# Two of the first four loads of a gated-attention and gMLP kernel asked for by ScalarE instead of SyncE

## The chip, the cores and the metric

The kernel runs on one core of a Trainium2 chip. The core has five engines with an instruction stream each: TensorE (PE in the profile, its weight loads PEld), VectorE (DVE), ScalarE (ACT), GpSimd (POOL) and SyncE (SP). All DMA transfers of the core share 16 DMA engines. The metric is the device time of one launch in microseconds (us), as the median of several runs.

## The reference

Two layers run one after the other. The first is a recurrence over 768 positions for 4 batches and 8 heads with a head width of 48:

```python
for t in range(S):
    state = alpha[:, :, t, :, None] * state + einsum('bhd,bhe->bhde', k[:, :, t], v[:, :, t])
    y[:, :, t] = einsum('bhd,bhde->bhe', q[:, :, t], state)
```

The second is a gated MLP with mixing over positions, on `x`, which is `y` with the heads laid side by side (768 positions of 384 numbers for each batch):

```python
h = maximum(x @ w_in, 0)                     # 384 -> 1024
u, v = h[..., :512], h[..., 512:]
v_n = (v - mean(v)) / sqrt(var(v) + 1e-6)    # over the 512
v_s = einsum('ts,bsd->btd', w_spatial, v_n) + b_spatial[None, :, None]
out = (u * v_s) @ w_out                      # 512 -> 384
```

Inputs and output are float32.

## The kernel before

The recurrence is computed in chunks of 128 positions, six to a batch, 24 in all. The first eight chunks are taken two at a time (`pair(j)`, for j from 0 to 3); the others go through `first(i)` one by one. For a pair, position 2p lies in the first half and position 2p+1 in the second half of partition p.

A pair begins with four loads, one each of `alpha` (tile `ac`), `k` (`kc`), `q` (`qc`) and `v` (`vc`), all through the inner function `load`. Each brings 384 KB, as rows of 96 numbers (384 bytes): 8 heads on 128 partitions. The tiles of a name rotate over three buffers. The steps of a pair that follow are:

- `ln` on ScalarE (L446) takes the logarithm of `ac` into `la`. It waits for the load of alpha.
- `cum` on TensorE (L455) sums the logarithms up to each position with a triangular matrix, into two PSUM banks.
- `einv` and `eexp` on ScalarE (L463, L472) take exp of minus the sums into `binvp` and exp of the sums in place.
- `ktf` (L477) multiplies `kc` by `binvp` into `kt`, twice, once for each half. In the first pair GpSimd does it. It waits for `binvp` and for the load of k.
- `qtf` on VectorE (L484) multiplies `qc` by exp of the sums into `qt`, twice. It waits for the load of q.
- `vbf` turns `vc` into bfloat16 (`vbp`), one half on GpSimd (L200) and one on ScalarE (L198), the lines of a copying helper. It waits for the load of v.
- TensorE transposes `qt` and `kt` (L505); VectorE and ScalarE copy the results to `kqT` (L200, L198).
- `upd` on TensorE (L539, L547) makes the state's increments from `kt` and `vbp`; VectorE then begins the state (L331), and ScalarE and GpSimd go on with it (L553, L338).
- The scores (L577), their masking on VectorE (L588) and the outputs (L604, L617) follow; the result goes through `x_sb` to `xT`, from which the second layer's matmuls (L822) start.

The order on each engine is written out by hand in the string `PLAN`. A word names an engine and an operation's number: P is TensorE, D is VectorE, A is ScalarE, G is GpSimd, S is SyncE, and Q marks the point at which a load has landed, which emits nothing. The function `replay` emits the operations in that order, and each engine works through its own list strictly. Numbers after a colon are columns of filler matmuls on the tile `junk` (L188), which TensorE runs ahead of the operation.

In `PLAN`, operations 34, 36, 38 and 40 are the issues of alpha, k, q and v for pair 0; 94, 96, 98 and 100 are those for pair 1; 42 is the first `ln`. All loads and stores are issued by SyncE, except the 1.5 KB of `b_spatial` by GpSimd. Completions of the loads are counted on eight semaphores in turn, so the ninth load waits on SyncE until the first has landed. The words around the change are:

```python
G32 S34 Q33 S36 G0 S38 S40 Q35 D1 Q37 S94 A42 D2 Q39 S96 P43:512:512:192 P53:64 A44 A45 G46
```

Ahead of the first `ln`, ScalarE has only the load of its function table (L171).

Of the kernel before, what the change touches and what calls it, by code (L numbers as in the profile page):

```python
# [54 lines left out]
LETTERS = {"P": "PE", "D": "DVE", "A": "ACT", "G": "POOL", "S": "SP", "Q": "DMA"}  # L55

PLAN = """
G32 S34 Q33 S36 G0 S38 S40 Q35 D1 Q37 S94 A42 D2 Q39 S96 P43:512:512:192 P53:64 A44 A45 G46 Q41 S98 A54 A55 D47 G56
D57 P51:512 Q95 P49 S100 P59:64 P61 A58 G48 D60 A50 D52 P63:192 Q97 S163 A62 P247 D65 A102 P71 D248 P74 D72 A64 Q99
S167 P103:96 G66 P113 D73 A104 A114 D68 D76 A115 Q101 P249 S165 G116 A105 A250 D117 G106 D107 P121:512 Q164 S169 D75  # L60
A122 P111:64 G67 P109 D112 P119 A110 G69 D120 Q168 S4 P131:192 D70 P134 G108 P77 G118 D133 G3 P123:128 A171 Q166
# [63 lines left out]
def kernel(  # L125
# [12 lines left out]
    nc = tc.nc  # L138
# [19 lines left out]
    LD, LP, WT, ST = 1.03, 1.46, 2.35, 0.8  # L158
# [129 lines left out]
    def op(key, *args, **kw):  # L288

        users = kw.pop("use", ())  # L290
        o = Op(key, *args, **kw)
        for s in users:
            s.users.append(o)
        ops.append(o)
        made[key] = o
        return o

    def got(*keys):
        return [made.get(x) for x in keys]

    def dma(key, us, emit, deps, prio, eng="SP", issue=0.99, lat=1.9):
        o = op(key + ("issue",), eng, issue, emit, deps, prio=prio)
        return op(key, "DMA", us, lambda _: None, [o], prio=prio, lat=lat)
# [102 lines left out]
    def io_users(x, j, back=None):  # L406

        j = j - IO if back is None else j
        if x == "cum":
            return got(("cum", 2 * j), ("cum", 2 * j + 1), ("cump", j, 0), ("cump", j, 1), ("updq", j))  # L410
        return got((x, 2 * j), (x, 2 * j + 1), (x + "p", j), (x + "p", j, 0), (x + "p", j, 1))
# [5 lines left out]
    def pair(j):  # L417

        st = T[2 * j]
        P = float(20 * j)  # L420
# [10 lines left out]
        def load(name, src):  # L431
            def emit(_):
                t = st[name] = io_pool.tile([128, 2, H, D], FP32, name=name).rearrange(
                    "p a h d -> p (a h d)").rearrange("p (h a d) -> p h a d", h=H, a=2)
                nc.sync.dma_start(  # L435
                    out=t.rearrange("p h a d -> p h (a d)"),
                    in_=src[b, :, t0:t0 + 2 * C, :].rearrange("h (p a) d -> p h (a d)", a=2))
            return emit

        for n, (x, src, u) in enumerate((("ac", alpha, "ln"), ("kc", k, "kt"), ("qc", q, "qt"), ("vc", v, "vb"))):  # L440
            dma((x, 2 * j), LP, load(x, src), io_users(u, j), P + 0.1 * n, issue=1.48)
            made[(x, 2 * j + 1)] = made[(x, 2 * j)]
            made[(x, 2 * j + 1, "issue")] = made[(x, 2 * j, "issue")]

# [650 lines left out]
    for b in range(B):  # L1095
        for c in range(NCH):
            i = b * NCH + c
            if i // 2 in PAIRS:
                if i % 2 == 0:
                    pair(i // 2)  # L1100
            else:
                first(i)
            second_v(b, c)
            if c == 2 or c == NCH - 1:
                for ft in range(NDS):
                    second_u(b, ft, c // 3)
        if b == 0:
            weights()
            bias()
        for th in range(2):  # L1110
            for dsl in range(NDS):
                second_s(b, dsl, th)
        for tt in range(NT):
            second_o(b, tt)
# [33 lines left out]
```

## Time and profile before

| | |
|---|---|
| median of 3 runs | 145.41 us (144.61 to 146.45) |
| span of the profiled execution, first to last instruction | 142.9 us |
| the profiled execution's own time | its span is what the page gives; 2.5 us less than the median of the runs |
| TensorE busy | 132.9 us (93%) |
| VectorE busy | 122.2 us (85%) |
| ScalarE busy | 108.2 us (76%) |
| GpSimd busy | 86.0 us (60%) |
| SyncE's DMA queue | 88944 packets, 28.32 MB, 92.0% of the 16 DMA engines |
| granted TensorE clock | 1.000 |

The span runs from the first to the last instruction of one profiled execution. The median comes from other executions and takes in what lies around the span. "Busy" adds up the time in which an engine had an instruction under way. A row of the timeline gives start, duration, engine, line of the kernel, operation, output and inputs, and in brackets how long the engine had been idle and what released it. In rows of DMA issues (SPq), the duration is that of the issuing; when the data has landed is told by the time to landing, counted from the start of the issue.

### The profile page before, as it was taken

How to read it: one execution, taken by the hardware profiler on the slowest of the kernel's cores; microseconds unless marked ns; L12 is line 12 of the kernel's file. 1: busy time of each engine (PE TensorE's matmuls, PEld its weight loads, DVE VectorE, ACT ScalarE, POOL GpSimd, SP SyncE). 2: the span in 40 equal slices, each digit the busy share in tenths (PEclk: the TensorE clock that was granted, in tenths of full speed). 3: DMA queues.
4: the chain of work that ended last, by engine and by line, in shares of the span. 5: the costliest groups of instructions: out<-in, count | busy, mean ns of one | idle time of the engine just before them, and what ended most of it. 6: DMA issues, size and time to landing. Idle time of an engine off the chain costs nothing.

```text
span 142.9 us, 4962 instructions
## 1 busy us (share of the span) xinstructions
PE 132.9 (93%) x1910; PEld 83.7 (59%) x1923; DVE 122.2 (85%) x290; ACT 108.2 (76%) x280; POOL 86.0 (60%) x147
## 2 busy tenths in 40 slices
PE   7978977999799999999999999999999999999990
PEld 3464857456465666665655666656666666556460
DVE  6759998998989799989789999889889989776950
ACT  3567398899976799999987889999878688760131
POOL 6945853748317999971288879910999994003700
PEclk9999999999999999999999999999999999999999
DMA  4999989999998999999899999999999103229645
GB/s 115 268 261 265 250 201 327 334 322 328 251 224 163 213 276 161 203 176 198 145 205 192 164 209 162 208 143 206 187 156 222 55 7 137 86 98 338 229 150 180
DMA packets 89000, 28.64 MB, mean 200 GB/s; under 512 B 83728, under 2 KB 87440, under 8 KB 88976
## 3 DMA queue, kind: packets, MB, share of 16 engines
q1 hardware_dynamic: 88944, 28.32, 92.0%
q8 instruction: 15, 0.25, 0.8%
q14 instruction: 9, 0.07, 0.2%
q0 software_dynamic: 32, 0.00, 0.0%
HBM read 23.60 MB, written 4.72 MB: 198 GB/s over the span
## 4 chain that ended last, share of the span: by engine, by line
PE 70%; DMA 10%; SPq 6%; ACT 6%; DVE 3%; issue 2%; ACTq 0%
PE bank L822 50%; DMA ac<-in_alpha_dram 10%; SPq L435 6%; PE bank L748 3%; PE bank L713 3%; PE bank L776 2%; PE bank L660 2%; ACT v_sb L204 2%; PE bank L734 2%; PE bank L770 2%; PE bank L392 2%; DVE stats L887 1%; DVE vn L919 1%; ACT x_sb L198 1%; PE bank L663 1%
## 5 line engine op out<-in xcount | busy, mean ns | idle before, releaser
L822 PE MATMUL bank<-w_spT,vn 128*128 128x384 bf16 x192 | 36.3, 326 | 0.0
L981 POOL TENSOR_TENSOR gT<-vsb,uT 128x384 bf16<-128x384 f32 x28 | 25.8, 928 | 14.2 <-DVE vsb L968 13.5
L822 PEld LDWEIGHTS <-vn 128*128 128x128 bf16 x192 | 16.8, 97 | 10.5 <-DVE vn L919 0.2
L684 POOL TENSOR_TENSOR kt<-kc,binv 128x384 bf16<-128x384 f32 x16 | 14.8, 924 | 12.6 <-ACT bc L679 6.6
L759 DVE TENSOR_TENSOR ptm<-bank,mask 128x512 bf16<-128x512 f32 x32 | 20.8, 683 | 0.6 <-PE bank L748 0.6
L822 PE MATMUL bank<-xT,w_in 128*128 128x384 bf16 x96 | 19.7, 326 | 0.1
L968 DVE TENSOR_TENSOR vsb<-bank,bsp_bc 128x384 f32<-128x384 f32 x31 | 16.6, 552 | 3.0 <-PE bank L822 1.6
L822 PE MATMUL bank<-w_out_sb,gT 128*128 128x384 bf16 (+1 forms) x100 | 18.6, 319 | 0.0
L822 PE MATMUL bank<-w_in,xT 128*128 128x512 bf16 x59 | 16.9, 379 | 1.1 <-issue 0.3
L198 ACT COPY kqT<-bank 128x512 bf16<-128x512 bf16 x26 | 14.8, 592 | 1.3 <-PE bank L713 0.8
L338 POOL TENSOR_TENSOR state<-state,bc 128x192 f32<-128x192 f32 x20 | 10.4, 518 | 8.8 <-ACT bc L553 6.4
L887 DVE BATCH_NORM_STATS2 stats<-v_sb 128x6 f32<-128x512 bf16 x20 | 13.7, 683 | 1.4 <-ACT v_sb L204 1.4
L198 ACT CAST x_sb<-bank 128x384 bf16<-128x384 f32 x24 | 11.5, 485 | 2.2 <-PE bank L776 1.9
L204 ACT ACTIVATE v_sb<-bank 128x512 bf16<-128x512 f32 x20 | 11.6, 601 | 1.6 <-PE bank L822 1.5
L822 PEld LDWEIGHTS <-gT 128*128 128x128 bf16 x100 | 8.9, 97 | 5.6 <-POOL gT L981 0.4
L200 POOL CAST sbd<-state 64x192 bf16<-64x192 f32 x32 | 10.9, 341 | 1.7
L822 PEld LDWEIGHTS <-w_in 128*128 128x128 bf16 x96 | 8.3, 97 | 5.3 <-issue 0.4
L198 ACT COPY xT<-bank 128x192 bf16<-128x192 bf16 (+1 forms) x25 | 8.7, 384 | 2.9 <-PE bank L392 2.6
L919 DVE TENSOR_SCALAR vn<-v_sb,mvs,rstd 128x512 bf16<-128x512 bf16 x24 | 9.8, 437 | 0.7 <-ACT rstd L912 0.7
L588 DVE TENSOR_TENSOR ptm<-bank,mask 128x512 bf16<-128x512 f32 x16 | 10.3, 676 | 0.0
L188 PE MATMUL bank<-junk 128*128 128x512 f32 (+4 forms) x24 | 9.3, 490 | 1.1 <-DVE junk L234 1.1
L200 DVE COPY kqT<-bank 128x512 bf16<-128x512 bf16 x22 | 9.0, 417 | 1.5 <-PE bank L505 0.9
(131 smaller groups left out, 288.2 us busy)
## 6 DMA issues: line engine op xcount, KB each, us to landing
ac<-in_alpha_dram SPq DMA_DIRECT2D x16, 192.0 KB, 4.6
qc<-in_q_dram SPq DMA_DIRECT2D x16, 192.0 KB, 4.7
kc<-in_k_dram SPq DMA_DIRECT2D x16, 192.0 KB, 4.8
vc<-in_v_dram SPq DMA_DIRECT2D x16, 192.0 KB, 4.3
raw_w<-in_moe_w_spatial_dram SPq DMA_DIRECT2D x3, 768.0 KB, 6.8
out_dram<-raw_w SPq DMA_DIRECT2D x11, 192.0 KB, 2.1
out_dram<-o_sb SPq DMA_DIRECT2D x9, 192.0 KB, 2.0
ac<-in_alpha_dram SPq DMA_DIRECT2D x4, 384.0 KB, 6.6
```

The costliest lines, as they stand in the source:

```text
L198: nc.scalar.copy(out=out, in_=in_)
L200: ENG[eng].tensor_copy(out=out, in_=in_)
L204: nc.scalar.activation(out=out, in_=in_, func=AF.Relu)
L338: ENG[eng].tensor_tensor(out=st["state"], in0=st["state"], in1=st["bc"][:, :, None].to_broadcast([128, HP, D]), op=ALU.mult)
L588: nc.vector.tensor_tensor(out=st[f"ptm{par}"][:, s], in0=st[f"pt{s}{par}"], in1=mask2[:, par], op=ALU.mult)
L684: ENG[eng].tensor_mul(out=k_blocks(kt3)[:, :, :, 0:D], in0=quad(st["kc"]), in1=st["binv"])
L759: nc.vector.tensor_tensor(out=st["ptm"][:, s], in0=st[f"pt{s}"], in1=mask4, op=ALU.mult)
L822: return lambda ps: nc.tensor.matmul(out=out(ps), lhsT=lhsT(), rhs=rhs(), start=start, stop=stop)
L887: nc.vector.bn_stats(out=stats, in_=d["v_sb"][:, tt, :])
L919: nc.vector.tensor_scalar(out=d["vn"][:, t, :], in0=d["v_sb"][:, t, :], scalar1=d["mvs"][:, t, 0:1], scalar2=d["rstd"][:, t:t + 1], op0=AL ...
L968: nc.vector.tensor_tensor(out=hold["vs"], in0=ps[:, 0:TH], in1=bsp_bc[:, th, :], op=ALU.add)
L981: ENG[eng].tensor_tensor(out=bt[b]["gT"][:, dsl, cols], in0=hold["vs"], in1=bt[b]["uT"][:, dsl, cols], op=ALU.mult)
```

## The change

The issues of q and v for pair 0 (operations 38 and 40) move from SyncE's list to ScalarE's, where they stand between the table load and the first logarithm. They carry no wait. The loads themselves keep their shape, source and destination. On SyncE the second pair's alpha follows the first pair's k directly. The landing of q is counted on the semaphore that k's landing had, and the other way round. The orders of TensorE, VectorE and GpSimd are unchanged, and lines behind the edit move down by one or two.

```diff
-G32 S34 Q33 S36 G0 S38 S40 Q35 D1 Q37 S94 A42 D2 Q39 S96 P43:512:512:192 P53:64 A44 A45 G46 Q41 S98 A54 A55 D47 G56
+G32 S34 Q33 S36 G0 A38 A40 Q35 D1 Q37 S94 A42 D2 Q39 S96 P43:512:512:192 P53:64 A44 A45 G46 Q41 S98 A54 A55 D47 G56
...
-                nc.sync.dma_start(
+                queue = nc.scalar if j == 0 and name in ("qc", "vc") else nc.sync
+                queue.dma_start(
                     out=t.rearrange("p h a d -> p h (a d)"),
                     in_=src[b, :, t0:t0 + 2 * C, :].rearrange("h (p a) d -> p h (a d)", a=2))
...
-            dma((x, 2 * j), LP, load(x, src), io_users(u, j), P + 0.1 * n, issue=1.48)
+            dma((x, 2 * j), LP, load(x, src), io_users(u, j), P + 0.1 * n, issue=1.48,
+                eng="ACT" if j == 0 and x in ("qc", "vc") else "SP")
```

## The prediction

> **What bounds the kernel now.** I read first the page's slices of the span, then the chain that ended last, then the timeline and the DMA rates of the first 40 us.
>
> ```profile
> PE   7978977999799999999999999999999999999990
> ...
> PEclk9999999999999999999999999999999999999999
> DMA  4999989999998999999899999999999103229645
> ```
>
> Each digit is a tenth of a slice of 3.6 us. From the eleventh slice (about 39 us) TensorE is full to the end. Only before that does it have holes, so a change in the loads can act only through the moment at which the full stretch begins. The chain agrees: from 38.80 us on it is TensorE with small pieces between. Ahead of that it runs over the loads of alpha, ScalarE and VectorE:
>
> ```profile
> 8.65 1.44 SPq L435
> 10.13 7.69 DMA ac<-in_alpha_dram
> 17.87 0.73 issue
> 18.75 0.38 ACT x_sb L198
> 19.17 6.97 DMA ac<-in_alpha_dram
> 26.17 0.84 ACT la L446
> ```
>
> A fixed 104.1 us (38.8 to 142.9) therefore follows whatever the first stretch becomes. How SP issues the first loads (start, duration):
>
> ```profile
> 0.74 0.43 SPq L435 DMA_DIRECT2D ac<-in_alpha_dram  x1
> 1.23 0.57 SPq L435 DMA_DIRECT2D kc<-in_k_dram  x1
> 1.85 1.00 SPq L435 DMA_DIRECT2D qc<-in_q_dram  x1
> 2.89 1.25 SPq L435 DMA_DIRECT2D vc<-in_v_dram  x1
> 4.18 1.45 SPq L435 DMA_DIRECT2D ac<-in_alpha_dram  x1
> ```
>
> The durations grow from 0.43 to 1.45 us for the same shape, so the later ones are not the price of an issue; they are waiting for room. The rates between 0 and 10 us (40 slices of 0.25 us) say for what:
>
> ```profile
> DMA  0000000278699999999999999999999999999999
> GB/s 0 0 0 0 0 0 0 74 126 178 192 324 323 327 323 306 278 262 260 258 263 261 261 263 261 258 263 261 263 263 257 264 260 263 261 261 261 260 261 264
> ```
>
> The engines are full from 2.75 us and settle at 261 GB/s. A load of 384 KB (393 thousand bytes) takes 1.5 us at that rate, the spacing of SP's issues. The transfers bound this stretch. The issues do not.
>
> **Landings now.** Issue times plus the times to landing of each row (3.6, 4.6, 5.5, 6.0 and 6.2 us) give alpha 4.3, k 5.8, q 7.4, v 8.9, and alpha of the second pair 10.4. Summing the rates gives 18 thousand bytes moved by 2.0 us, 223 by 3.0, 543 by 4.0, 613 by 4.25, and 261 more per us afterwards. Alpha has moved at 3.5 and k at 4.9, so a landing is 0.8 to 0.95 us after its last byte.
>
> **What moves.** Instruction orders of TensorE, VectorE and GpSimd are unchanged. SP loses two issues. ScalarE gets two, behind its table load (0.73 to 2.01) and ahead of the first logarithm, with no wait on either. Behind them stands all of ScalarE's order, beginning with the logarithm, which now starts at 4.43 after 2.42 us of waiting for alpha. The two issues cost about 0.43 + 0.57 by SP's first two rows, or 1.25 + 1.45 by its blocked ones. From 2.01 at the latest they end between 3.0 and 4.7. I take the low end, since ScalarE's ring is empty. The high end would delay the logarithm by 0.3.
>
> On SP, alpha and k of the second pair move up behind the first pair's alpha and k. SP gains no time from this that the transfers can use: they are full already.
>
> **Order of transfers, the costly part.** Four loads that went one after the other now come from two rings. The Trainium skill, "DMA: Bandwidth & Descriptors", section "Issuing engines are not separate DMA queues", speaks against the change: the engine that issues does not matter, all run on the same 16 DMA engines and interleave, and only sequencer time is saved. By SP's row alone one would book 1.00 + 1.25 us of issue saved; by the rule, with the full DMA row, zero. I take the rule's zero, and price the interleaving at equal shares.
>
> When does ScalarE's ring begin? No row shows a DMA issue behind a table load. The bounds are 0.75 us (the issue doesn't wait for the table) and 2.01 us (it does). The same skill, "Perfetto Trace Analysis", section "Sequencer Loop", has the sequencer hand an engine's instruction to a queue and read on, which puts it at the early end. Nearest row: SP's first issue is followed by bytes 1.0 us later. I take the early end, with one SP issue of 0.43 ahead of it: first bytes of q at about 2.2 us, when alpha has moved some 45 thousand bytes. Then, with equal shares:
> - alpha is through at 45 + 2 x 348 = 741 moved, at 4.74 us, landing 5.6 (now 4.3)
> - q at 393 + 438 = 831, 5.1 us, landing 6.0 (now 7.4)
> - k at 786 + 741 = 1527, 7.75 us, landing **8.65** (now 5.8), since half of the bandwidth after alpha goes to q and v
> - v at 786 + 831 = 1617, landing 9.0 (now 8.9)
> - alpha of the second pair at 1179 + 786 = 1965, landing 10.4, as now.
>
> So q is early, k is late by 2.8 us, and from the fifth load on nothing moves.
>
> **What a late k does.** Ahead of `ktf` GpSimd does not wait for k today; binv releases it at 6.49.
>
> ```profile
> 6.49 1.78 POOL L477 TENSOR_TENSOR kt<-kc,binvp 128x384 bf16<-128x384 f32 x2
> ...
> 7.49 1.02 DVE L484 TENSOR_TENSOR qt<-qc,bank 128x384 bf16<-128x384 f32 x2 [0.85 <-DMA qc<-in_q_dram]
> ...
> 8.93 0.50 POOL L200 CAST vbp<-vc 128x384 bf16<-128x384 f32 x1 [0.67 <-DMA vc<-in_v_dram]
> ...
> 10.49 0.36 DVE L331 COPY state<-bank 128x192 f32<-128x192 f32 x1 [0.53 <-PE bank L547]
> ```
>
> It would start at 8.7, 2.2 us late, and end at 10.5 instead of 8.3. TensorE transposes the second kt at 8.78 now and had 0.45 us to spare, so it is at 10.6, late by 1.8. Its state update (9.89) goes to 11.7 and VectorE's first state copy from 10.49 to 12.3. The early q gains nothing: its cover, the waits of 0.85 (q) and 0.67 (v), disappears into the wait for k. The late logarithm (+1.25) lies beside the late k and adds nothing: binv would be there at 7.6.
>
> From 10.49 to 21.14 VectorE is busy 10.07 of 10.65 us, in a fixed order, with 0.17 us of shown wait. The delay passes through. ScalarE's wait of 1.99 us for the third alpha at 17.85 absorbs ScalarE's share, but not VectorE's or TensorE's order. Behind that VectorE's waits in the timeline are 0.18 (22.81), 0.23 (32.32) and 0.22 (34.21); I count 0.45 of these as absorbing. At 38.8 the delay is 1.8 - 0.45 = 1.35, plus 0.05 of pieces lost later: **+1.4 us**. The profiled execution has a span of 142.9 us, 2.5 below the median of 145.41 and below the fastest run, 144.61; I put the difference on the median: 146.8.
>
> **Rivals.**
> - **Late start.** The issue waits for the table. First bytes of q come at 3.2, when 277 have moved. Alpha lands at 4.75, k at 7.8, v at 9.9. v decides now: its cast on GpSimd and ScalarE moves by 1.0, the state update too; less 0.45 gives +0.6: 146.0. For it: the table load is the only thing before. Against: the rule above.
> - **Alternation by whole loads**, the same as no visible effect. The skill's DMA page, section "Queues, rings and completion order", has an engine drain a packet of up to 64 descriptors before it changes rings, and 1024 rows on 16 engines are 64 each. Then the order is alpha, q, k, v: k lands at 7.4, kt starts 0.9 late, less 0.45 on TensorE and most of the rest behind: +0.1, 145.5. Against: the trace's packets average 376 B (2.11 MB in 5614), single rows.
> - **Two rings run faster.** Between 2.75 and 3.75 us the rate is 324 GB/s, against 261 when SP is blocked, and from 1.75 to 2.75 the engines are half empty. If two rings held 324, the first 1.57 MB would save 1.2 us, and k would be late by 1 us at most. VectorE's full stretch leaves little of a gain: 0.4 us, at most 0.9 if later loads also come earlier: 144.5 to 145.0. Against: the full DMA row at 261.
> - **ScalarE is held in its issue**, on the other side. By the skill's "Perfetto Trace Analysis", section "DMA Instruction — HWDGE (DVE, Sync)", a descriptor generator is locked for one issue at a time, and the lock wait counts as issue. SP has six loads with no semaphore ahead of it; its blocked issues (1.45 us each) would hold the lock. If ScalarE gets through only after them, at about 8 to 9 us, the logarithm starts 4 to 5 us late and everything with it: +4, less 0.9 of the waits named: about +3.1 to 4.1, 149. It decides once v's issue ends after 8.2 us (then more than 2.9 us reach the end). For it: SP's rows are back to back. Against: 0.05 us gaps between them, and SP's own first issues are short.
>
> **How the numbers follow.** Equal shares from the start 0.38, late start 0.19, whole loads 0.15, faster rings 0.12, held issue 0.16. The range takes in the rivals from the mild gain to the held issue: 144.8 to 149.2. Two per cent is 2.9 us, about what a measurement of this kernel can tell from no change. Slower by more than that is the held issue plus a tail of the first case (0.25), faster by more needs later loads to follow too (0.06), and 0.69 lies within.
>
> **What would show it.** Right: two ScalarE issues before 3.5 us, k landing at about 8 to 9, GpSimd's kt waiting for k, VectorE's first state copy near 12.3, alpha of the second pair still near 10.4, the full TensorE stretch starting 1 to 1.5 us late. Wrong: k before 7 us; rates over 300 GB/s between 4 and 8 us; the logarithm behind a long ScalarE issue; a TensorE clock below full in the first slices, which the gaps in its work do not suggest.

## The result, and the profile after

| | before | with the change |
|---|---|---|
| median of 4 runs each (before: one run more than in the table above) | 145.49 us (144.61 to 146.45) | 147.34 us (147.13 to 147.79) |
| ratio, 95% interval | | 1.0136 [1.0106, 1.0165] |
| span of the profiled execution | 142.9 us | 146.0 us |
| that execution's own time | 144.61 us, its fastest | 147.79 us, its slowest |

The change costs 1.85 us: slower, by less than 2%. The two profiles differ by 3.1 us in span, but one is the fastest execution of its kernel and the other the slowest of its own, so the medians decide the size and the profiles tell where. In every execution the time is 1.7 to 1.8 us above the span. The ratios here and below leave out a few disturbed executions that the ranges contain. The difference of 2.5 us that the prediction put on the median was 1.7 us of surroundings and 0.8 us of a fast execution.

The profile after, slices of the span (here 3.65 us each), the rows that answer to those of before:

```profile
PE   7759986999979999999999999999999999999990
...
PEclk9999999999999999999999999999999999999999
DMA  4999999975998989979999999998999302319635
```

TensorE has more holes in the second and third slices than before. Its last wait, read below from the timeline, ends 2.4 us later. The granted clock stays full. What happens in the first stretch shows in the timeline (start, duration, engine, line, operation; in brackets how long the engine had been idle and what released it):

```profile
0.73 1.28 ACT L171 ACT_TABLE_LOAD   x1 [0.73 <-PEq L1134]
0.74 0.42 SPq L436 DMA_DIRECT2D ac<-in_alpha_dram  x1
0.76 0.49 ACTq L436 DMA_DIRECT2D qc<-in_q_dram  x1
...
1.22 0.57 SPq L436 DMA_DIRECT2D kc<-in_k_dram  x1
...
1.28 0.67 ACTq L436 DMA_DIRECT2D vc<-in_v_dram  x1
...
5.54 0.84 ACT L448 ACTIVATE la<-ac 128x768 bf16<-128x768 f32 x1 [3.52 <-DMA ac<-in_alpha_dram]
...
8.98 1.78 POOL L479 TENSOR_TENSOR kt<-kc,binvp 128x384 bf16<-128x384 f32 x2 [2.57 <-ACT bank L474]
9.83 0.51 ACT L198 CAST vbp<-vc 128x384 bf16<-128x384 f32 x1 [0.97 <-DMA vc<-in_v_dram]
9.94 0.40 PE L507 MATMUL bank<-ident,kt 128*128 128x128 bf16 x4 [0.95 <-POOL kt L479]
...
12.53 0.36 DVE L331 COPY state<-bank 128x192 f32<-128x192 f32 x1 [0.53 <-PE bank L549]
```

Both ScalarE issues lie within the table load and are short. Alpha is late: the logarithm starts at 5.54 instead of 4.43. GpSimd's `kt` starts at 8.98 instead of 6.49. The row names ScalarE as the releaser, but by its rows ScalarE had made both halves of `binvp` by 8.35; k landed at 8.81, so k is what came last. VectorE's first state copy is at 12.53 instead of 10.49, **2.04 us late**.

Landings, as issue plus time to landing:

| us | alpha | k | q | v | alpha, second pair |
|---|---|---|---|---|---|
| before | 4.3 | 5.8 | 7.4 | 8.9 | 10.4 |
| forecast with the change | 5.6 | 8.65 | 6.0 | 9.0 | 10.4 |
| measured with the change | 5.45 | 8.81 | 6.24 | 9.81 | 10.67 |

The DMA rates of the first 10 us after the change, in slices of 0.25 us:

```profile
DMA  0000000384799999999999999999999999999999
GB/s 0 0 0 0 0 0 0 80 81 52 177 263 258 312 329 324 330 301 266 258 263 264 255 265 260 261 258 263 264 255 260 258 269 258 260 263 263 263 261 257
```

Two rings settle at the same 261 GB/s as one. They start slower: up to 3.5 us the slices add up to 306 thousand bytes, against 386 before.

### The profile page after: what moved, and what is told of

It reads as the page before. It is cut to its first block, busy times and chain, and to the rows that moved or that the text cites. A ratio compares the mean times of both kernels' runs of the same rounds, so it can differ in the third digit from the quotient of the medians.

```text
span 146.0 us, 4962 instructions
## 1 busy us (share of the span) xinstructions
PE 134.0 (92%) x1910; PEld 84.3 (58%) x1923; DVE 123.4 (85%) x290; ACT 108.8 (75%) x280; POOL 85.9 (59%) x147
## 4 chain that ended last, share of the span: by engine, by line
PE 58%; DVE 13%; POOL 9%; DMA 7%; issue 5%; ACT 4%; SPq 2%; POOLq 0%; ACTq 0%; DVEq 0%
PE bank L824 40%; DMA vc<-in_v_dram 7%; DVE ptm L590 3%; PE bank L750 2%; POOL kt L479 2%; DVE sbd L200 2%; PE bank L715 2%; PE bank L778 2%; POOL mask L256 2%; PE bank L772 2%; PE bank L662 2%; PE bank L736 2%; SPq L642 2%; PE bank L392 1%; ACT binvp L465 1%
## 5 line engine op out<-in xcount | busy, mean ns | idle before, releaser
L479 POOL TENSOR_TENSOR kt<-kc,binvp 128x384 bf16<-128x384 f32 x7 | 6.3, 910 | 7.2 <-ACT binvp L465 3.6
L590 DVE TENSOR_TENSOR ptm<-bank,mask 128x512 bf16<-128x512 f32 x16 | 10.4, 679 | 0.0
```

The source lines that it names most:

```text
L590: nc.vector.tensor_tensor(out=st[f"ptm{par}"][:, s], in0=st[f"pt{s}{par}"], in1=mask2[:, par], op=ALU.mult)
```

## The experiments

All kernels are the kernel before with the words of `PLAN` that each diff shows; where a load goes to ScalarE, the test in `load` names that load alone. Each group is compared with runs of the kernel before on the same chip. The state copy meant below is VectorE's first (10.49 in the profile of before, 10.57 in a second one).

**Is a late k enough, without a second queue?** `e1_k_last` keeps one queue and asks for k last.

```diff
-G32 S34 Q33 S36 G0 S38 S40 Q35
+G32 S34 Q33 S38 G0 S40 S36 Q35
```

> All four loads of the first pair on SyncE again, in the order alpha, q, v, k: k should land at about 8.9 us as it did with the change, while alpha lands at 4.3 as before and ScalarE issues nothing. Late-k theory: GpSimd's kt starts at about 8.95 waiting for k, VectorE's first state copy at about 12.5, time 1.4 to 2.2 us over before (about 147.2). Rival (the second queue or the late logarithm costs the time): q and v are earlier, alpha is not late, so no change from before (within 0.3 us).

Measured: 150.81 us (147.13 to 151.74, 4 runs) against 145.37: far more than the late k. Three of the four executions had a granted clock of 0.954 to 0.966; the fourth, at 1.000, took 147.13, which is 1.8 above before. TensorE by stretches of the profiled execution (window: its length, PE busy and count, granted clock, DMA share, GB/s):

```profile
5.00:10.00 5.00, 2.32 (x13) 1.00 1.27 261
10.00:15.00 5.00, 4.53 (x90) 0.64 1.27 261
15.00:20.00 5.00, 5.00 (x19) 0.50 1.23 258
20.00:30.00 10.00, 8.12 (x191) 0.84 0.98 279
```

With alpha on time and k at 9.1, TensorE had nothing to do for 2.1 us ahead of its first transpose of `kt`. Only 2.32 of 5 us were busy, and behind the hole the clock fell to half and stayed there for some ten microseconds. That is a second effect on top of the late k. `e9_k_last_filled` puts filler matmuls ahead of that transpose.

```diff
-P51:512 Q95 P49 S100
+P51:512 Q95 P49:512:384 S100
```

> One queue, order alpha, q, v, k, with fillers of 512 and 384 columns (about 1.8 us) ahead of the first kt transpose, where TensorE sat idle from 8.1 to 10.3 and its granted clock then fell to 0.5. Idle-hole theory: clock back to 1.0 in all runs and 1.5 to 2.2 us over before, about 147.2, against 150.8 without filler. Rival (the slow clock has another cause, or filler doesn't count as work): clock stays below 0.97 and time near 150.8.

Measured: 147.18 us (146.63 to 147.69), ratio 1.0137 [1.0076, 1.0197], clock 1.000 in all four. Its timeline:

```profile
9.03 1.78 POOL L477 TENSOR_TENSOR kt<-kc,binvp 128x384 bf16<-128x384 f32 x2 [2.62 <-DMA kc<-in_k_dram]
...
12.59 0.36 DVE L331 COPY state<-bank 128x192 f32<-128x192 f32 x1 [0.53 <-PE bank L547]
```

This is the main result. One queue, no issue on ScalarE, alpha at 4.3 as before, k at 8.9: `kt` and the state copy stand where they stand in the change (8.98, 12.53), and so does the ratio (1.0136). The order in which the bytes arrive explains the loss without the second queue. The one execution of e1 at a full clock, 147.13, agrees. The three others of e1 took 3.6 to 4.6 us more than that one, and none of e9's four did: with so few executions this speaks strongly, but not finally, for the hole as the cause of the low clock.

**Does the change itself suffer from a slow TensorE?** `e8_change_filled` puts filler into both of its holes.

```diff
-Q39 S96 P43:512:512:192 P53:64
+Q39 S96 P43:512:512:192:448 P53:64
...
-P51:512 Q95 P49 S100
+P51:512 Q95 P49:384 S100
```

> The change with TensorE's two new holes filled: 448 columns ahead of the first sums (5.5 to 6.4) and 384 ahead of the first kt transpose (9.0 to 9.9). Late-k theory: the chain from k's landing at 8.8 stays, so still 1.4 to 2 us over before. If instead most of the change's loss is a slow TensorE behind its holes, no more than 0.7 us over before.

Measured: 147.82 us (147.34 to 149.68), ratio 1.0170 [1.0103, 1.0238], state copy at 12.43. Nothing is won back, so a slow TensorE is not the change's loss. In the change the late alpha also delays `qt`, and so the hole ahead of `kt` is 0.95 us, not 2.1.

**One load alone on ScalarE's queue.** Each of these three moves one issue from S to A.

```diff
-G32 S34 Q33 S36 G0 S38 S40 Q35
+G32 S34 Q33 A36 G0 S38 S40 Q35     (e3_k_on_act)
+G32 S34 Q33 S36 G0 A38 S40 Q35     (e5_q_on_act)
+G32 S34 Q33 S36 G0 S38 A40 Q35     (e6_v_on_act)
```

> k alone goes to ScalarE's queue; alpha, q and v stay on SyncE. The second queue, its issue ahead of the logarithm and alpha's sharing remain (alpha at about 5.4), but k shares with alpha and lands at about 6.2. Late-k theory: no wait of GpSimd for k, first state copy about 11.1, time 0.1 to 0.6 us over before. Rival (second queue costs the time by itself): about 1.9 us over before, as the change.

> q alone goes to ScalarE's queue, v stays on SyncE behind k. Equal-share theory: alpha 5.4, q 6.2, then k has the engines to itself and lands at about 7.7, v at 9.2; kt starts at 7.8, first state copy about 11.4, time 0.3 to 0.8 us over before. Rival (queues are not shared equally; k waits for all that ScalarE's queue holds or is not held up at all): k at 6 or at 8.8, and the time of before or of the change.

> v alone goes to ScalarE's queue, q stays on SyncE behind k. Equal shares give alpha 5.4, v 6.2, k 7.7, q 9.2. Here it is q that comes last: qt waits for q until 9.2, TensorE's first transposes start at about 9.8 instead of 8.1, first state copy at about 12.3, time 1.2 to 2 us over before. Rival (only k's landing counts): as with q alone on ScalarE's queue, first state copy about 11.3, 0.7 to 1.2 us over before.

| | alpha | k | q | v | state copy | median, us | ratio |
|---|---|---|---|---|---|---|---|
| e3, k alone | 5.33 | 6.15 | 7.54 | 9.06 | 11.03 | 146.60 | 1.0070 [1.0033, 1.0107] |
| e5, q alone | 5.29 | 7.49 | 6.15 | 9.00 | 11.22 | 146.24 | 1.0085 [1.0044, 1.0126] |
| e6, v alone | 5.34 | 7.54 | 9.04 | 6.19 | 12.48 | 147.29 | 1.0125 [1.0075, 1.0175] |

The landings are those that equal shares forecast, although the bytes are shared less evenly, as the next section shows. The load that shares its start with alpha lands at about 6.2, alpha moves from 4.4 to 5.3, and what SyncE has behind alpha comes in at about 7.5 and 9.0. In e6 the late load is q; it landed at 9.04, just ahead of this `qt`, though the row names ScalarE:

```profile
9.17 1.02 DVE L486 TENSOR_TENSOR qt<-qc,bank 128x384 bf16<-128x384 f32 x2 [2.53 <-ACT bank L474]
...
12.48 0.36 DVE L331 COPY state<-bank 128x192 f32<-128x192 f32 x1 [0.53 <-PE bank L549]
```

A late q costs about as much as a late k: the state copy waits for the last of the loads that the first transposes need. The rival that only k's landing counts falls. e3 cost more than its state copy tells (+0.5) and more than was expected. Its ten runs lie between 145.22 and 147.25 at a full granted clock, and the profiled one was the fastest.

**Order alone, one queue.** `e4_q_before_k` asks in the order alpha, q, k, v; `e2_k_first` in the order k, alpha, q, v.

```diff
-G32 S34 Q33 S36 G0 S38 S40 Q35
+G32 S34 Q33 S38 G0 S36 S40 Q35     (e4_q_before_k)
+G32 S36 Q33 S34 G0 S38 S40 Q35     (e2_k_first)
```

> One queue, order alpha, q, k, v: k lands at 7.4 instead of 5.9, nothing else is late. This is what the change would have been had each engine taken whole loads from its two queues in turn. kt starts about 1.0 us later than before, first state copy at about 11.0 to 11.1, time 0 to 0.5 us over before; if a late k acts in full from the first microsecond, 1 us over before.

> One queue, order k, alpha, q, v: only alpha is late (5.85 instead of 4.3, slightly more than with the change). Late-k theory: a late logarithm alone costs 0.4 to 0.8 us, since the waits of VectorE for q and of GpSimd for v take up part of it; first state copy at about 11.5. Rival (late logarithm carries the change's loss): 1.5 to 2 us over before, first state copy at 12.3 or later.

e4: k at 7.47, state copy at 11.19 (+0.70), 145.78 us, ratio 1.0056 [1.0014, 1.0098]. A small delay is passed on too, where up to 0.5 was expected.

e2: k early and alpha 1.5 us late, 146.80 us, ratio 1.0099 [1.0067, 1.0131], above what was expected. The logarithm starts at 5.96, but the state copy at 12.64 (+2.15). By these rows the rest is TensorE's pace:

```profile
6.86 0.48 PE L455 MATMUL bank<-la,le_pair 128*128 128x384 bf16 x1 [1.38 <-ACT la L446]
...
8.41 1.92 PE L188 MATMUL bank<-junk 128*128 128x512 f32 x2
```

In the profile of before that filler pair took 1.02 us. Behind 1.4 us without work TensorE ran at about half pace, although the granted clock is given as 1.00 for that stretch.

**Is the spread of e3 a hole of the same kind?** `e7_k_on_act_filled` is e3 with `P43:512:512:192:448`.

> k alone on ScalarE's queue, as in the run before, with one filler matmul of 448 columns more ahead of the first sums, about 0.9 us, which fills TensorE's hole while alpha is late (5.3 to 6.3). Idle-hole theory: the wide spread of that version (145.2 to 147.3) comes from TensorE falling to half speed after the hole in some executions; with the hole filled all runs lie near its fastest, 145.2 to 146.0, 0 to 0.3 us over before. Rival (the spread comes from the transfers of two queues): spread and median as without filler, about 146.6.

Measured: 146.04 us (145.28 to 148.53, 10 runs), ratio 1.0042 [1.0002, 1.0081]. Eight executions lie between 145.28 and 146.35, closer together than e3's; the other two, at a granted clock of 0.977, took 148.0 and 148.5. The filler itself ran long, and the state copy was at 11.42 against e3's 11.03. Inconclusive.

**Is there something to win in the kernel before?** `e10_before_filled` only puts filler (`P51:512:320`) into its one hole.

> The kernel before with 320 columns of filler more in TensorE's hole ahead of the first transposes (7.2 to 8.1 us). If that hole puts TensorE's clock at risk before the change too, the median falls by 0.2 to 0.5 us and the slowest executions (granted clock 0.988 to 0.997) go away. If not, no change (within 0.2 us).

Measured: 145.32 us (144.13 to 146.65, 10 runs), ratio 0.9997 [0.9965, 1.0030]. No gain; no version tried beats the kernel before.

**Both kernels again on one chip**, to see whether the shift repeats.

> The kernel before unchanged, for a second profiled execution: the first one was the fastest of its runs (span 142.9, the others mostly 143.3 to 143.7). VectorE's first state copy at 10.4 to 10.6, GpSimd's first kt at 6.5 released by binvp and not by k, and a span near 143.5.

> The change unmodified, for a second profiled execution and a narrower interval: first state copy at 12.4 to 12.6, 1.7 to 2.2 us over before. If the delay at the first state copy is passed on whole, the span is longer than that of the second profile of before by 1.9 to 2.3 us; if 0.45 us of it is absorbed on the way as predicted, by 1.4 to 1.6.

Measured: before 144.93 us (one run, span 143.2); the change 147.07 us (146.74 to 147.67), ratio 1.0124 [1.0083, 1.0166], span 145.9. Landings in e12 are alpha 5.63, q 6.42, k 8.96, v 9.82. The state copy is at 12.69 against 10.57 in e11, 2.12 us late. TensorE's last wait in the first stretch ends at 41.27 against 39.07, 2.20 late, and in between VectorE is 1.9 to 2.9 late. The spans differ by 2.7 us, more than either case expected, but e12's profile is the slowest of its four executions. No part of the delay is lost on the way to 41 us.

## Why the prediction was right or wrong

**Right: the issues. Wrong: the start of ScalarE's transfers.** ScalarE issued at 0.76 and 1.28 for 0.49 and 0.67 us. The issue does not wait for the table load (0.73 to 2.01). The logarithm started at 5.54, when alpha was there, so the rival of a held issue falls. But the bytes did not follow at the forecast 2.2 us. Packets and MB of the two rings (q1 is SyncE's, q10 ScalarE's), first up to 3 us and then from 3 to 5 us:

```profile
q1 hardware_dynamic: 417, 0.16, 27.9%
q10 hardware_dynamic: 8, 0.00, 0.4%
...
q10 hardware_dynamic: 908, 0.35, 70.3%
q1 hardware_dynamic: 657, 0.25, 47.1%
```

Only 8 packets of q had moved by 3.0 us. In the six other profiles with a load on ScalarE (e3, e5 to e8, e12) it was 23 to 44. The start is nearer to the 3.2 us of the late-start rival, although the issue is early. Whether the table load or something else holds the transfers is not shown.

**Right in the sum, in part by luck: equal shares.** From 3 to 5 us ScalarE's ring moved 0.35 MB and SyncE's 0.25. Only from 6 to 8 us were the shares equal (0.26 each). A late start and a larger share worked against each other, and so alpha, q and k landed within 0.25 us of the forecast (k at 8.81 against 8.65). Whole-load alternation would have brought k at 7.4, and 324 GB/s was not held; the rate is 261 with one ring or two. v came 0.8 us after its forecast and alpha of the second pair 0.3. The 80 thousand bytes that were missing at 3.5 us are 0.3 us at 261 GB/s, which is an estimate and leaves half a microsecond of v's lateness open: from 8.5 to 9.5 us ScalarE's ring moved only 0.02 MB and SyncE's 0.24. Neither decided: the state's update, which reads v's casts, stood behind the transposes of `kt` until 11.93, and ScalarE's cast of v had started at 9.83.

**Right: the late k decides.** `kt` at 8.98 (forecast 8.7), state copy at 12.53 (12.3). Experiment e9 shows that this delay alone, with one queue, gives the whole ratio. Two per cent was called about what can be told from no change; with these runs 1.4% could be told.

**Mis-sized: the absorbing term.** The forecast was +1.4 and the medians differ by 1.85. A first part of what was missing is the state copy, which was 2.04 late and not 1.8. The other is the step "I count 0.45 of these as absorbing", by which 1.35 should have been left at 38.8. (TensorE is full from that row on. The digit of the eleventh slice, which the prediction named, is still 7.) This is TensorE's last wait of the first stretch, before and after:

```profile
38.80 0.35 PE L834 MATMUL bank<-ident,w_row 64*128 64x64 bf16 x12 [0.63 <-DVE w_row L200]
...
41.17 0.35 PE L836 MATMUL bank<-ident,w_row 64*128 64x64 bf16 x12 [0.80 <-DVE w_row L200]
```

It came 2.37 us late, in the second pair of profiles 2.20, and in e9 2.18 (at 40.98). On balance nothing was absorbed up to there. Yet the waits did shrink as the prediction had it: over 25.5 us from its state copy on, VectorE's idle time fell from 1.56 to 1.06 us, by 0.50. But its busy time rose from 23.94 to 24.44, by the same 0.50. Some of its casts took another time than before. Before:

```profile
20.20 0.52 DVE L200 CAST sbd<-state 64x192 bf16<-64x192 f32 x2
...
20.73 0.91 POOL L477 TENSOR_TENSOR kt<-kc,binvp 128x384 bf16<-128x384 f32 x1 [1.09 <-ACT x_sb L198]
...
24.78 0.87 DVE L200 CAST w_in<-raw_w 128x512 bf16<-128x512 f32 x1
...
29.64 0.73 DVE L200 CAST w_in<-raw_w 128x512 bf16<-128x512 f32 x2
```

After:

```profile
22.24 1.25 DVE L200 CAST sbd<-state 64x192 bf16<-64x192 f32 x2
...
22.47 0.91 POOL L479 TENSOR_TENSOR kt<-kc,binvp 128x384 bf16<-128x384 f32 x1 [0.80 <-ACT binvp L465]
...
27.45 0.42 DVE L200 CAST w_in<-raw_w 128x512 bf16<-128x512 f32 x1
...
31.86 1.34 DVE L200 CAST w_in<-raw_w 128x512 bf16<-128x512 f32 x2
```

Of the first two casts, 0.26 us each before, the second alone now took 0.98. It became due just as GpSimd had begun `kt` for the third pair, and ended about 0.1 us after it. Before, GpSimd began only when both casts were through. The Trainium skill, "SBUF — State Buffer", section "Who interferes with whom", states that VectorE's fast copies and casts share a pair of ports with GpSimd, and that whichever starts first holds it for its whole instruction while the other stands still. By that rule the second cast waits for the 0.91 us of `kt`, and these rows fit. The pair takes as long in the profiles of e12 and of e2 to e9, all delayed, and 1.43 us in e1.

It is not the only one. VectorE is 2.04 us late ahead of this cast and 2.76 behind it. It is back at 2.27 behind the first `w_in`, which had been the long one before, at 2.84 behind the second pair of `w_in`, and at 2.20 behind the waits that the prediction counted. Which casts are long differs between profiles of one kernel too: the first `w_in` took 0.43 us in e11, where the kernel is that of before.

In e10, which is not slower than before, the long `sbd` cast stands as well. There VectorE's lateness of 0.31 us rises to 1.05 with it and is back at 0.33 at 33 us: the slack pays for the cast (later casts, of `vn`, bring the lateness to 0.9 by 42 us in that profile). So the slack can be spent once. In the change it pays for the longer casts, and nothing is left for the late k. This reading is argued from rows. No run put the casts out of GpSimd's way while k stayed late.

**Half right: the late logarithm "adds nothing".** In the change k is later still, and e9, with alpha on time, costs the same. But on its own a late alpha is not free: it cost 1.0% in e2, where TensorE lost its pace.

**The clock.** The prediction said that the gaps in TensorE's work do not suggest a clock below full. That held for the change, by less of a margin than it sounded: e1 lost its clock with a hole of 2.1 us where the change has one of 0.95.

**Left open.** Why e3 spreads over 2 us; what delays the first bytes of ScalarE's ring; and why the two pairs of profiles gain another 0.7 and 0.5 us between TensorE's last wait and the end, when the medians differ by no more than 1.85 and 1.81.

## What to carry to other kernels

Here the transfers were at their full rate, and a second queue added nothing; it shared out the rate. Loads that were due one after the other were then late at the head of the first queue by what the second queue took, and a load helped nobody by coming before the last one that the same step needs. So list for each of the first loads when its consumer is otherwise ready, ask in that order on one queue, and count slack behind a delay only once: check whether a shifted order makes two engines meet that did not meet before.

## What the runs showed of the hardware beyond expectation

- A hole of 2.1 us in TensorE's work (2.32 of 5 us busy) was followed by a granted clock of 0.50 for some ten microseconds in the profile of e1; three of its four executions had a lowered mean clock (0.954 to 0.966) and took 3.6 to 4.6 us more than the fourth. With filler matmuls (e9) all four stood at 1.000. The Trainium skill, "TensorE: Matmul & The Clock Gate", section "What's actually happening", puts the fall to half rate after an idle window of about 3.4 us; here a shorter hole was enough.
- In e2, TensorE ran at about half pace behind 1.4 us of idle time with the granted clock given as 1.00.
- A DMA issue on ScalarE is taken while its function table loads (0.76 us, load from 0.73 to 2.01), but by 3.0 us only 8 of its packets had moved, against 417 of SyncE's, whose first issue came at 0.74.
- Two rings on the same 16 DMA engines did not share them equally throughout: 0.35 MB against 0.25 from 3 to 5 us, 0.26 each from 6 to 8, 0.02 against 0.24 from 8.5 to 9.5.
- A VectorE cast of 0.26 us took 0.98 us where a GpSimd instruction of 0.91 us had begun just ahead of it.
- Transfers started slower when loads came from two queues: 306 thousand bytes up to 3.5 us in the change, 312 and 328 in e12 and e8, 340 to 357 with one load on ScalarE (e3, e5, e6, e7), against 356 to 400 in seven profiles with one queue.
